# Output tiles of 128 tokens, and row pairs of w2 and m2 on one partition

## The chip, the cores and the metric

One core of a Trainium2 chip runs the whole kernel: TensorE (PE) multiplies, VectorE (DVE), ScalarE (ACT) and GpSimd (POOL) do the rest, SyncE (SP) issues most transfers between HBM and the core's 128-partition SBUF. The metric is device time in microseconds (us) of one execution, lower being better.

## The reference

Three parts follow each other. Attention of 32 packed queries over 576 tokens, then of the tokens over the packed result (4 batches, 8 heads of 64). Then a mixture of 4 experts with dense routing on the 2304 tokens x of width 512. Then a "soft" mixture: every token is spread over 32 slots, 8 experts work on 4 slots each, and each token reads the slots back.

```python
# x: (2304, 512) after attention; w1: (4,512,1024), w2: (4,1024,512)
p = domain_probs / (domain_probs.sum(-1, keepdims=True) + 1e-09)
for e in range(4):
    h = np.maximum(x @ w1[e], 0.0)
    out += p[:, e:e + 1] * (h @ w2[e])
x = out
# phi: (512, 32), m1: (8,512,1024), m2: (8,1024,512)
logits = x @ phi
d = softmax(logits, over tokens)
slot_input = (d.T @ x).reshape(8, 4, 512)
for e in range(8):
    h = np.maximum(slot_input[e] @ m1[e], 0.0)
    slot_out[e] = h @ m2[e]
c = softmax(logits, over slots)
return c @ slot_out          # (2304, 512)
```

All arrays are float32. In the kernel, m1 and m2 are the last part's `moe2_w1` and `moe2_w2`.

## The kernel before

The main loop computes the hidden layer h of the first mixture, 256 of its 1024 columns at a time, and never forms x: since slot_input is linear in h, h's columns are summed over tokens with the weights d (into `tacc`, 32 slots x 1024 columns x 4 experts), and w2 is applied to those sums alone. phi is folded into w2 beforehand (`wphi`). This loop ends at about 444 us; d's weights for the last batch and the last sums end at about 457 us.

What follows works on 32 slots, so it has little arithmetic and much weight to read:

- `tacc` is transposed (L961), and its two halves are added into `tt` (L973, L974).
- si = tt times w2 (L989), over 16 chunks of 512 KB.
- si is scaled and transposed (`sit`, L1007); hid = relu(si times m1) (L1026), over 32 chunks. `hidt` (L1047) transposes hid.
- so = hid times m2 (L1074): for the first four experts in all 512 output columns, over 16 chunks of 512 KB; for the last four in two parts (PARTS: 384 output columns, then 128), over 16 chunks of 384 KB and 4 of 512 KB.
- For each part, so is added up (L1094), spread by a selection matrix (`sr`, L1096), split into a rounded value and its remainder (`rr`, L1098, L1099), and multiplied with the turned c (`ct`) to give output rows (`o`, L1112). The PSUM results are drained by ACT and DVE in turn (L1065) into SBUF tiles `ob`, each stored by one DMA (L1119).

All weights of this end come as one list, `chunks` (L663 to L686): w2, m1, m2. Each chunk goes into the next of a ring of slots (4 KB per partition; some were `hn`, the main loop's buffer, and are named so in the trace, others are `ck`). `load_chunk` issues chunk after chunk on SP's queue in the order of the list, as slots come free: SP waits until the reader of the slot's former chunk is done. The output tiles take further slots of the same ring, and their stores come behind all chunks on SP's queue; the last one goes by ACT's queue.

`turn_c` (L637) makes ct. It is stepped once after each four chunks of hid's loop (L1037), so that its work lies between hid's matmuls: a matmul spreads a batch's 32-token blocks to 128 partitions, ACT rounds them into ct, and DVE writes the remainder on half of the partitions.

In the kernel before, an output tile is one batch's 96 rows r, of 6 tokens j each (token 6 r + j of the batch). A block x of 32 tokens (one of NBLK = 18) holds the tokens 18 t + x, so ct's row r = 3 t + y, and turn_c writes its columns with a step of 3. The order around the change is that of the code, by hand: nothing is scheduled.

Of the kernel before, what the change touches and what calls it, by code (L numbers as in the profile page):

```python
# [9 lines left out]
F32 = mybir.dt.float32  # L10
F32R = mybir.dt.float32r
AF = mybir.ActivationFunctionType
ALU = mybir.AluOpType
# [5 lines left out]
def tile_packed_attention_moe_softmoe(  # L19
# [21 lines left out]
    NBLK = S // 32  # L41
# [7 lines left out]
    EPS = 1e-9  # L49
    CHUNK = 1024  # L50
    PARTS = ((0, 384), (384, 128))
    NJ = NBLK // 3
    XC = CHUNK // 256
    HT_BUFS = 5
    NR = 5
# [49 lines left out]
    def tr_ps(name):  # L105
        turns["tr"] += 1
        return ps_tr[turns["tr"] % 2].tile([128, 512], F32, tag="tr", name=name)
# [529 lines left out]
    def turn_c(ct):  # L637
        cf = soft.tile([128, S], F32, tag="sx", name="cf", bufs=2).rearrange(
            "p (x t) -> p x t", t=32
        )  # L640
        dve.transpose(out=cf, in_=c_sb)
        for b in range(NB):
            own = slice(32 * b, 32 * b + 32)
            for y0, ny in ((0, 2), (2, 1)):
                m = ny * NJ * 32
                ps = tr_ps(f"ct{b}{y0}")
                pe.matmul(
                    ps[:, :m], fold[own].rearrange("p c t -> p (c t)"),
                    cf[own, NJ * y0 : NJ * (y0 + ny), :],
                    start=True, stop=True, tile_position=(32 * b, 0),  # L650
                )
                src = ps[:, :m].rearrange("p (y j t) -> p y j t", y=ny, t=32)
                dst = ct[:, b].rearrange("p j (t y) -> p y j t", y=3)[:, y0 : y0 + ny]
                for y in range(ny):
                    act.copy(dst[:, y], src[:, y])
                    for r in (slice(32, 64), slice(96, 128)):
                        dve.tensor_tensor(
                            out=dst[r, y], in0=src[r, y],
                            in1=dst[r, y].bitcast(F32), op=ALU.subtract,
                        )  # L660
                yield

    chunks = []  # L663
    for x in range(0, NFT, 2):
        for e in range(NE):
            chunks.append(
                w2[e, 128 * x : 128 * x + 256, :].rearrange("(x p) d -> p x d", p=128)
            )
    for s in range(NX // 4):
        for dc in range(NDC):  # L670
# [2 lines left out]
    for x in range(0, NFT, 2):  # L673
        for e in range(4):
            chunks.append(
                m2[e, 128 * x : 128 * x + 256, :].rearrange("(x p) d -> p x d", p=128)
            )
    for d0, dw in PARTS:
        nx = CHUNK // dw
        for x in range(0, NFT, nx):  # L680
            for e in range(4):
                chunks.append(
                    m2[4 + e, 128 * x : 128 * (x + nx), d0 : d0 + dw].rearrange(
                        "(x p) d -> p x d", p=128
                    )
                )  # L686
    chunk_t = {}
    slots = []
# [48 lines left out]
    with tc.manual_schedule():  # L737
# [214 lines left out]
        for t in st2:  # L952
            pool.memset(t, 0.0)
        tt = wphi
        ct = fin.tile([128, NB, NJ, 96], F32R, name="ct")
        for i in range(2):
            ps, ps2 = tr_ps(f"tt{i}a"), tr_ps(f"tt{i}b")
            for j in range(4):
                o = 128 * (4 * (2 * i + j // 2) + j % 2)
                for el in range(2):  # L960
                    pe.transpose(  # L961
                        (ps if j < 2 else ps2)[:, 256 * (j % 2) + 128 * el :][:, :128],
                        tacc[:, o + 256 * el : o + 256 * el + 128],
                        ident,
                    )
            for k, t in enumerate((ps, ps2)):
                t = t.rearrange("p (j l r q) -> p r j l q", j=2, l=2, r=2)
                both = tt[:, 4 * i + 2 * k : 4 * i + 2 * k + 2, :].rearrange(
                    "p j (a l s) -> p j l a s", a=2, l=2
                )  # L970
                for el in range(2):
                    dst = both[:, :, el]
                    act.copy(dst, t[:, 0, :, el].rearrange("p j (a s) -> p j a s", a=2))  # L973
                    dve.tensor_tensor(  # L974
                        out=dst, in0=t[:, 1, :, el].rearrange("p j (a s) -> p j a s", a=2),
                        in1=dst, op=ALU.add,
                    )
# [65 lines left out]
        for i in range(2):  # L1043
            ps = tr_ps(f"hidt{i}")
            for j in range(4):
                o = 512 * i + 128 * j
                pe.transpose(ps[:, 128 * j : 128 * j + 128], hid[:, o : o + 128], ident)  # L1047
            for s in range(2):
                (act.copy if i else dve.tensor_copy)(
                    hm[s][:, 4 * i : 4 * i + 4, :, 4 * s : 4 * s + 4].rearrange(  # L1050
                        "p a b c -> p (a b) c"
                    ),
                    ps.rearrange("p (a c) -> p a c", c=32)[:, :, 4 * s : 4 * s + 4],
                )
# [35 lines left out]
        for d0, dw in PARTS:  # L1090
            so = mm_ps(f"so{d0}")
            project(so, 1, dw)
            h = slice(d0, d0 + dw)
            dve.tensor_tensor(out=so_sb[:, h], in0=so[:, :dw], in1=so_sb[:, h], op=ALU.add)  # L1094
            sr = tr_ps(f"sr{d0}")
            pe.matmul(sr[:, :dw], sel, so_sb[:, h], start=True, stop=True)  # L1096
            rr = fin.tile([128, dw], F32R, name=f"rr{d0}")
            act.copy(rr, sr[:, :dw])  # L1098
            dve.tensor_tensor(  # L1099
                out=rr[64:128], in0=sr[64:128, :dw], in1=rr[64:128].bitcast(F32),  # L1100
                op=ALU.subtract,
            )
            nb, nt = 512 // dw, min(CHUNK // dw, NJ)
            for b in range(NB):
                rows = out[b * S : (b + 1) * S, h].rearrange("(r j) d -> r j d", j=NJ)
                for j0 in range(0, NJ, nt):
                    ob = out_tile()
                    for j in range(j0, j0 + nt, nb):
                        m = min(nb, j0 + nt - j)
                        ps = mm_ps(f"o{d0}_{b}_{j}")  # L1110
                        for jl in range(m):
                            pe.matmul(  # L1112
                                ps[:96, dw * jl : dw * jl + dw], ct[:, b, j + jl, :], rr,
                                start=True, stop=True,
                            )
                        drain(
                            ob[:96, dw * (j - j0) : dw * (j - j0 + m)], ps[:96, : dw * m]
                        )
                    (act if (d0, b) == (PARTS[-1][0], NB - 1) else sp).dma_start(  # L1119
                        rows[:, j0 : j0 + nt, :],  # L1120
                        ob[:96, : dw * nt].rearrange("p (j d) -> p j d", d=dw),
                    )


# [28 lines left out]
```

## Time and profile before

| | |
|---|---|
| Time, median of 3 runs | 549.1 us (548.97 to 549.73) |
| The profiled execution's own time | 549.31 us |
| its span, first to last instruction | 547.2 us |
| PE busy | 498.7 us, 91% |
| DVE, ACT, POOL busy | 322.2, 240.0, 236.3 us |
| moved by DMA | 104.06 MB, of which 4.72 MB written |

The busy shares are means over stages with different limits. Nearly all of PE's work lies in the main loop; the stage after it is read from its own stretch. A row of the view by stage has, after the stretch, its length, busy time and count for each engine, then TensorE's granted clock, the DMA engines' busy share and the rate. A share can read a little over 1, since packets overlap.

### The profile page before, as it was taken

To read this page: it belongs to the slowest core of one execution; us is meant where nothing else is said; L and a number is where in the kernel's file an instruction comes from. 1 tells how busy PE (TensorE), PEld (TensorE's weight loads), DVE (VectorE), ACT (ScalarE), POOL (GpSimd) and SP (SyncE) were. 2 spreads that over 40 slices of the span, in tenths; PEclk is the share of its full clock that TensorE was granted. 3 is DMA by queue.
4 is the path that set the end of the run, shared out by engine and by line. 5 is a ranking of instruction groups with operands and counts; after the bars stand their busy time and mean duration, and the time that the engine had idled before them with its cause. 6 is when DMAs were issued, how large, how long until landed. Compare 5 with 4: busy or idle time off the path is not lost.

```text
span 547.2 us, 12839 instructions
## 1 busy us (share of the span) xinstructions
PE 498.7 (91%) x5356; PEld 347.5 (63%) x5356; DVE 322.2 (59%) x623; ACT 240.0 (44%) x548; POOL 236.3 (43%) x246
## 2 busy tenths in 40 slices
PE   7898999989999999899998989999999977998882
PEld 5776787867865767687556768775787853222132
DVE  6475457776767776768776676666645434451051
ACT  3766564655452447365334654551454411120041
POOL 8212445676642557675335555842555612000000
PEclk9998999999999999999999999999999997998998
DMA  8997155352430443443205432360388369999998
GB/s 283 365 375 271 49 166 176 98 166 79 153 122 1 146 143 103 150 148 120 79 10 177 158 100 79 132 234 22 126 277 292 128 238 398 409 389 383 371 253 239
DMA packets 70874, 104.06 MB, mean 190 GB/s; under 512 B 4433, under 2 KB 50257, under 8 KB 70817
## 3 DMA queue, kind: packets, MB, share of 16 engines
q1 hardware_dynamic: 66992, 93.20, 49.2%
q0 software_dynamic: 3232, 9.75, 6.0%
q8 instruction: 42, 0.69, 0.5%
q10 hardware_dynamic: 592, 0.29, 0.2%
q14 instruction: 16, 0.12, 0.1%
HBM read 98.52 MB, written 4.72 MB: 189 GB/s over the span
## 4 chain that ended last, share of the span: by engine, by line
PE 54%; DVE 15%; DMA 14%; ACT 8%; issue 4%; POOL 3%; SPq 0%; POOLq 0%; DVEq 0%; ACTq 0%
PE h L473 26%; DMA ck<-in_moe_w_dram 7%; PE sl L611 6%; PE g L443 5%; PE lg L500 4%; DMA hn<-in_moe_w_dram 3%; DVE pkt L366 3%; PE sb L297 3%; ACT etm L336 3%; DMA k<-in_k_dram 3%; PE sa L297 2%; PE w2t L251 2%; DVE hn L483 2%; POOL hn L484 2%; PE pw L237 1%
## 5 line engine op out<-in xcount | busy, mean ns | idle before, releaser
L473 PE MATMUL h<-a,g 128*128 128x288 f32 x1536 | 227.6, 302 | 6.9 <-DVE g L455 4.5
L473 PEld LDWEIGHTS h<-a,g 128*128 128x128 f32 x1536 | 208.7, 188 | 33.4 <-issue 22.3
L484 POOL TENSOR_TENSOR hn<-hn,dp_sb 128x576 f32<-128x576 f32 x128 | 152.0, 1193 | 130.0 <-DVE hn L483 126.3
L477 ACT ACTIVATE ht<-h 128x288 f32<-128x288 f32 x256 | 103.7, 412 | 155.2 <-PE h L473 154.9
L483 DVE STREAM_TRANSPOSE hn<-ht 128x576 f32<-128x576 f32 x128 | 96.3, 758 | 50.2 <-ACT ht L477 50.0
L455 DVE TENSOR_TENSOR g<-g,g 128x512 fp32r<-128x512 f32 x64 | 41.1, 683 | 24.8 <-ACT g L454 24.8
L611 PE MATMUL sl<-hn,dpt 32*32 32x512 f32 x1152 | 48.2, 597 | 2.4 <-DVE dpt L572 2.0
L454 ACT CAST g<-g 128x512 fp32r<-128x512 f32 x64 | 34.3, 588 | 21.1 <-PE g L443 21.0
L500 PE MATMUL lg<-ht,wphi 128*32 128x288 f32 x512 | 37.8, 412 | 0.0
L443 PE MATMUL g<-w,gl 64*32 64x512 f32 x512 | 35.7, 601 | 0.4 <-ACT ht L477 0.2
L611 PEld LDWEIGHTS sl<-hn,dpt 32*32 32x32 f32 x1152 | 21.0, 103 | 22.3 <-issue 13.3
L500 PEld LDWEIGHTS lg<-ht,wphi 128*32 128x32 f32 x512 | 13.5, 109 | 32.7 <-issue 25.5
L366 DVE COPY pkt<-gl 32x32 f32<-32x32 f32 x64 | 22.8, 356 | 7.3 <-ACT gl L357 6.5
L346 PE MATMUL pv<-etm,v 128*64 128x64 f32 x468 | 19.0, 225 | 6.5 <-ACT etm L336 3.4
L410 POOL TENSOR_TENSOR a<-a,a 64x576 fp32r<-64x576 f32 x14 | 20.0, 1427 | 9.6 <-ACT a L409 8.8
L336 ACT COPY etm<-et 32x288 f32<-32x288 f32 x52 | 22.2, 428 | 1.6 <-DVE et L330 0.4
L346 PEld LDWEIGHTS pv<-etm,v 128*64 128x64 f32 x468 | 16.2, 137 | 10.6 <-ACT etm L336 5.7
L1074 PE MATMUL so<-hn,tacc 128*32 128x384 f32 (+1 forms) x80 | 18.5, 590 | 2.7 <-DMA hn<-in_moe_w_dram 2.5
L629 DVE TENSOR_TENSOR tacc<-sl,tacc 128x512 f32<-128x512 f32 (+2 forms) x32 | 15.3, 545 | 9.4 <-PE sl L611 9.4
L297 PE MATMUL sa<-k,pt 128*128 128x288 f32 x56 | 16.9, 428 | 3.7 <-DVE k L288 3.6
L256 ACT COPY hn<-w2t 128x512 f32<-128x512 f32 x32 | 17.3, 588 | 6.6 <-PE w2t L251 6.5
L251 PE MATMUL w2t<-ident,hn 128*128 128x128 f32 x128 | 18.3, 287 | 1.8 <-ACT hn L256 1.3
(180 smaller groups left out, 492.4 us busy)
## 6 DMA issues: line engine op xcount, KB each, us to landing
w<-in_moe_w_dram SPq DMA_DIRECT2D x32, 1024.0 KB, 5.4
hn<-in_moe_w_dram SPq DMA_DIRECT2D x42, 512.0 KB, 9.7
ck<-in_moe_w_dram SPq DMA_DIRECT2D x42, 512.0 KB, 8.0
hn<-in_moe_w_dram SPq DMA_DIRECT2D x14, 384.0 KB, 8.5
q<-in_q_dram POOLq DMA_DIRECT2D x12, 288.0 KB, 3.2
out_dram<-ob SPq DMA_DIRECT2D x11, 288.0 KB, 4.4
k<-in_k_dram POOLq DMA_DIRECT2D x10, 288.0 KB, 3.2
v<-in_v_dram POOLq DMA_DIRECT2D x10, 288.0 KB, 3.6
```

Of the source, the lines that this page charges most:

```text
L297: pe.matmul(ps[:, :HS], lhs[:, j, :], t[:, :, j, :], start=(j == 0), stop=(j == 1))
L336: act.copy(etb[hf % len(etb)][r, h % 2, :, 32 * (h // 2) : 32 * (h // 2) + 32], et[r, HB * hf : HB * hf + HB, :],)
L346: pe.matmul(pv[64 * par : 64 * par + 64, :64], vn[:, x, :], etb[hf % len(etb)][:, par, x, :], start=(hf == 0 and x == 0), stop=(hf == 1 an ...
L366: dve.tensor_copy(pkb[32 * h : 32 * h + 32, dh, o : o + 32], glb[src : src + 32, 2 * g + h // 2, :],)
L443: pe.matmul(pss[g][32 * ((c + 2 * g) % 4) : 32 * ((c + 2 * g) % 4) + 32, :], gl[b % 2][r, c, :], t[r, c], start=True, stop=True, tile_posi ...
L455: dve.tensor_tensor(out=lo, in0=pss[g], in1=hi.bitcast(F32), op=ALU.subtract)
L473: pe.matmul(ps[:, :HS], gg[:, l, g, e % 2, fs], r[:, ts], start=(g == 0 and t == 0), stop=(g == 1 and t == 2),)
L477: act.activation(out=ht[:, ts], in_=ps[:, :HS], func=AF.Relu)
L483: dve.transpose(out=own, in_=unturned.pop((n, kf, e)).rearrange("p (x t) -> p x t", t=32))
L484: pool.tensor_tensor(out=own, in0=own, in1=dp_sb[:, n // NU, :, e].unsqueeze(2).to_broadcast([128, NBLK, 32]), op=ALU.mult,)
L500: pe.matmul(lg_t[b, pr][32 * c : 32 * c + 32, :HS], wphi[:, 2 * i + kf, 32 * e : 32 * e + 32], ht_t[n, kf, e][:, HS * hf : HS * hf + HS], ...
L611: pe.matmul(pss[f][c : c + 32, :], dpt[r, x, :], hn[r, p0 : p0 + NU, x, 2 * ep : 2 * ep + 2].rearrange("p n e k f -> p n (e k f)"), start= ...
```

## The change

The diff does three things.

1. An output tile holds 128 rows: 32 tokens t of each of the 4 batches, for a fixed x; partition 32 b + t of tile x is token 18 (32 b + t) + x. ct is laid out as 18 blocks of 128 columns, and `turn_c` makes it in pieces of 9 blocks instead of 12 and 6. There are 18 blocks instead of 24 for the last matmuls; a stored tile has 2 blocks of 384 columns or 6 of 128 (OUT_X).
2. In a chunk of w2 or m2, partition p holds rows next to each other in HBM (w2: rows 2 p and 2 p + 1 of the chunk's 256; m2: two of the rows 8 p to 8 p + 7, or all eight of them for the 128-column part), instead of rows p and p + 128.
3. The transposes of tacc and hid take their columns with a step of 2 and of 8, so that the same rows meet.

```diff
--- before.py
+++ after.py
@@ -49,7 +49,7 @@
     EPS = 1e-9
     CHUNK = 1024
     PARTS = ((0, 384), (384, 128))
-    NJ = NBLK // 3
+    OUT_X = {384: 2, 128: 6}
     XC = CHUNK // 256
     HT_BUFS = 5
     NR = 5
@@ -641,30 +641,28 @@
         dve.transpose(out=cf, in_=c_sb)
         for b in range(NB):
             own = slice(32 * b, 32 * b + 32)
-            for y0, ny in ((0, 2), (2, 1)):
-                m = ny * NJ * 32
-                ps = tr_ps(f"ct{b}{y0}")
+            for x0 in range(0, NBLK, HB):
+                m = HB * 32
+                ps = tr_ps(f"ct{b}{x0}")
                 pe.matmul(
                     ps[:, :m], fold[own].rearrange("p c t -> p (c t)"),
-                    cf[own, NJ * y0 : NJ * (y0 + ny), :],
+                    cf[own, x0 : x0 + HB, :],
                     start=True, stop=True, tile_position=(32 * b, 0),
                 )
-                src = ps[:, :m].rearrange("p (y j t) -> p y j t", y=ny, t=32)
-                dst = ct[:, b].rearrange("p j (t y) -> p y j t", y=3)[:, y0 : y0 + ny]
-                for y in range(ny):
-                    act.copy(dst[:, y], src[:, y])
-                    for r in (slice(32, 64), slice(96, 128)):
-                        dve.tensor_tensor(
-                            out=dst[r, y], in0=src[r, y],
-                            in1=dst[r, y].bitcast(F32), op=ALU.subtract,
-                        )
+                src = ps[:, :m].rearrange("p (x t) -> p x t", t=32)
+                dst = ct[:, x0 : x0 + HB, own]
+                act.copy(dst, src)
+                for r in (slice(32, 64), slice(96, 128)):
+                    dve.tensor_tensor(
+                        out=dst[r], in0=src[r], in1=dst[r].bitcast(F32), op=ALU.subtract
+                    )
                 yield
 
     chunks = []
     for x in range(0, NFT, 2):
         for e in range(NE):
             chunks.append(
-                w2[e, 128 * x : 128 * x + 256, :].rearrange("(x p) d -> p x d", p=128)
+                w2[e, 128 * x : 128 * x + 256, :].rearrange("(p x) d -> p x d", x=2)
             )
     for s in range(NX // 4):
         for dc in range(NDC):
@@ -673,16 +671,16 @@
     for x in range(0, NFT, 2):
         for e in range(4):
             chunks.append(
-                m2[e, 128 * x : 128 * x + 256, :].rearrange("(x p) d -> p x d", p=128)
+                m2[e].rearrange("(p x) d -> p x d", x=NFT)[:, x : x + 2, :]
             )
     for d0, dw in PARTS:
         nx = CHUNK // dw
         for x in range(0, NFT, nx):
             for e in range(4):
                 chunks.append(
-                    m2[4 + e, 128 * x : 128 * (x + nx), d0 : d0 + dw].rearrange(
-                        "(x p) d -> p x d", p=128
-                    )
+                    m2[4 + e, :, d0 : d0 + dw].rearrange("(p x) d -> p x d", x=NFT)[
+                        :, x : x + nx, :
+                    ]
                 )
     chunk_t = {}
     slots = []
@@ -952,15 +950,15 @@
         for t in st2:
             pool.memset(t, 0.0)
         tt = wphi
-        ct = fin.tile([128, NB, NJ, 96], F32R, name="ct")
+        ct = fin.tile([128, NBLK, 128], F32R, name="ct")
         for i in range(2):
             ps, ps2 = tr_ps(f"tt{i}a"), tr_ps(f"tt{i}b")
             for j in range(4):
-                o = 128 * (4 * (2 * i + j // 2) + j % 2)
                 for el in range(2):
+                    o = 512 * (2 * i + j // 2) + 256 * el
                     pe.transpose(
                         (ps if j < 2 else ps2)[:, 256 * (j % 2) + 128 * el :][:, :128],
-                        tacc[:, o + 256 * el : o + 256 * el + 128],
+                        tacc[:, o : o + 256].rearrange("p (f x) -> p x f", x=2)[:, j % 2],
                         ident,
                     )
             for k, t in enumerate((ps, ps2)):
@@ -1043,8 +1041,11 @@
         for i in range(2):
             ps = tr_ps(f"hidt{i}")
             for j in range(4):
-                o = 512 * i + 128 * j
-                pe.transpose(ps[:, 128 * j : 128 * j + 128], hid[:, o : o + 128], ident)
+                pe.transpose(
+                    ps[:, 128 * j : 128 * j + 128],
+                    hid.rearrange("p (f x) -> p x f", x=NFT)[:, 4 * i + j],
+                    ident,
+                )
             for s in range(2):
                 (act.copy if i else dve.tensor_copy)(
                     hm[s][:, 4 * i : 4 * i + 4, :, 4 * s : 4 * s + 4].rearrange(
@@ -1100,26 +1101,23 @@
                 out=rr[64:128], in0=sr[64:128, :dw], in1=rr[64:128].bitcast(F32),
                 op=ALU.subtract,
             )
-            nb, nt = 512 // dw, min(CHUNK // dw, NJ)
-            for b in range(NB):
-                rows = out[b * S : (b + 1) * S, h].rearrange("(r j) d -> r j d", j=NJ)
-                for j0 in range(0, NJ, nt):
-                    ob = out_tile()
-                    for j in range(j0, j0 + nt, nb):
-                        m = min(nb, j0 + nt - j)
-                        ps = mm_ps(f"o{d0}_{b}_{j}")
-                        for jl in range(m):
-                            pe.matmul(
-                                ps[:96, dw * jl : dw * jl + dw], ct[:, b, j + jl, :], rr,
-                                start=True, stop=True,
-                            )
-                        drain(
-                            ob[:96, dw * (j - j0) : dw * (j - j0 + m)], ps[:96, : dw * m]
+            nb, nt = 512 // dw, OUT_X[dw]
+            rows = out[:, h].rearrange("(p x) d -> p x d", x=NBLK)
+            for x0 in range(0, NBLK, nt):
+                ob = out_tile()
+                for x in range(x0, x0 + nt, nb):
+                    m = min(nb, x0 + nt - x)
+                    ps = mm_ps(f"o{d0}_{x}")
+                    for xl in range(m):
+                        pe.matmul(
+                            ps[:, dw * xl : dw * xl + dw], ct[:, x + xl, :], rr,
+                            start=True, stop=True,
                         )
-                    (act if (d0, b) == (PARTS[-1][0], NB - 1) else sp).dma_start(
-                        rows[:, j0 : j0 + nt, :],
-                        ob[:96, : dw * nt].rearrange("p (j d) -> p j d", d=dw),
-                    )
+                    drain(ob[:, dw * (x - x0) : dw * (x - x0 + m)], ps[:, : dw * m])
+                (act if d0 and x0 + nt == NBLK else sp).dma_start(
+                    rows[:, x0 : x0 + nt, :],
+                    ob[:, : dw * nt].rearrange("p (x d) -> p x d", d=dw),
+                )
 
 
 # ---- launch: one core; inputs and outputs as the reference has them ----
```

The order of the instructions moves in three places. On SP's queue before, near the end of the chunk list (the second number of a shape is rows per partition, `hn` and `ck` are slots):

```order
L715 DMA hn<-in_moe_w_dram 128x2x512 x4
L715 DMA ck_5750<-in_moe_w_dram 128x2x512 x2
L715 DMA ck_5753<-in_moe_w_dram 128x2x512 x2
L715 DMA ck_5784<-in_moe_w_dram 128x2x512 x2
L715 DMA ck_5787<-in_moe_w_dram 128x2x512
L715 DMA ck_5807<-in_moe_w_dram 128x2x512
L715 DMA ck_5809<-in_moe_w_dram 128x2x512 x2
L715 DMA hn<-in_moe_w_dram 128x2x512 x2
L715 DMA hn<-in_moe_w_dram 128x2x384 x14
```

and the same place after:

```order
L713 DMA hn<-in_moe_w_dram 128x1024 x4
L713 DMA ck_5750<-in_moe_w_dram 128x1024 x2
L713 DMA ck_5753<-in_moe_w_dram 128x1024 x2
L713 DMA ck_5784<-in_moe_w_dram 128x1024 x2
L713 DMA ck_5787<-in_moe_w_dram 128x1024
L713 DMA ck_5804<-in_moe_w_dram 128x1024
L713 DMA ck_5806<-in_moe_w_dram 128x1024 x2
L713 DMA hn<-in_moe_w_dram 128x1024 x2
L713 DMA hn<-in_moe_w_dram 128x2x384 x14
```

Counts and order are the same; the first 16 chunks of m2 are now one run of 1024 elements per partition, those of 384 columns keep two runs.

On SP's queue before, the output stores that follow the chunks (`ob` and `hn` are output tiles):

```order
L1119 DMA out_dram<-ob_6021 96x2x384
L1119 DMA out_dram<-ob_6029 96x2x384
L1119 DMA out_dram<-ob_6037 96x2x384
L1119 DMA out_dram<-hn 96x2x384 x4
L1119 DMA out_dram<-ob_6073 96x2x384 x2
L1119 DMA out_dram<-ob_6088 96x2x384 x2
L1119 DMA out_dram<-ob_6103 96x2x384
L1119 DMA out_dram<-ob_6103 576x1x128
L1119 DMA out_dram<-ob_6161 576x1x128
L1119 DMA out_dram<-ob_6173 576x1x128
```

and after:

```order
L1117 DMA out_dram<-ob_6009 128x2x384
L1117 DMA out_dram<-ob_6017 128x2x384
L1117 DMA out_dram<-ob_6025 128x2x384
L1117 DMA out_dram<-hn 128x2x384 x4
L1117 DMA out_dram<-ob_6061 128x2x384 x2
L1117 DMA out_dram<-ob_6115 128x6x128 x2
```

Fifteen stores from 96 partitions become eleven from 128; in the 128-column part before, the tokens of a batch form one list of 576 rows.

On ACT, before, its half of the drains of the 128-column part, with the last store on its own queue:

```order
L1098 CAST rr_6147<-sr_6145 128x128
L1065 COPY ob_6103<-o_0_0_6150 96x512
L1065 COPY ob_6161<-o_1_0_6162 96x512
L1065 COPY ob_6173<-o_2_0_6174 96x512
L1065 COPY ob_6185<-o_3_0_6186 96x512
L1119 DMA out_dram<-ob_6185 576x1x128
```

and after:

```order
L1099 CAST rr_6112<-sr_6110 128x128
L1066 COPY ob_6115<-o_0_6116 128x512
L1066 COPY ob_6115<-o_6_6127 128x512
L1066 COPY ob_6138<-o_12_6139 128x512
L1117 DMA out_dram<-ob_6138 128x6x128
```

Four pieces of 512 columns become three, and the last store stands behind the third.

## Rows read from the trace of the kernel before

**Rows 1.** The page, 40 equal slices: busy tenths of the DMA engines and GB/s.
```profile
DMA  8997155352430443443205432360388369999998
GB/s 283 365 375 271 49 166 176 98 166 79 153 122 1 146 143 103 150 148 120 79 10 177 158 100 79 132 234 22 126 277 292 128 238 398 409 389 383 371 253 239
```

**Rows 2.** Chain of waits, 420 to 548 us: start us, length us, what.
```profile
464.64 7.36 DMA ck<-in_moe_w_dram
...
513.47 8.48 DMA ck<-in_moe_w_dram
...
534.26 4.36 DMA out_dram<-ob
```

**Rows 3.** Busy time by stage, the last two columns being DMA share and GB/s.
```profile
464.00:480.00 16.00, 14.75 (x122) 4.76 (x118) 6.26 (x21) 2.01 (x5) 2.17 (x2) 1.00 1.03 409
482.00:502.00 20.00, 18.47 (x131) 5.67 (x130) 7.88 (x19) 3.91 (x10) 0.00 (x0) 0.91 1.05 387
505.00:518.00 13.00, 11.12 (x52) 2.53 (x56) 0.00 (x0) 0.59 (x1) 0.00 (x0) 1.00 1.07 373
522.00:526.00 4.00, 2.39 (x12) 0.67 (x12) 0.90 (x2) 0.48 (x1) 0.00 (x0) 1.00 1.00 257
530.00:540.00 10.00, 7.46 (x101) 5.34 (x99) 5.37 (x13) 4.95 (x11) 0.00 (x0) 1.00 0.98 291
541.00:546.00 5.00, 0.00 (x0) 0.00 (x0) 0.00 (x0) 0.00 (x0) 0.00 (x0) 0.64 0.86 221
```

**Rows 4.** DMA issues from 447 to 522 us: count, KB each, median us to landing.
```profile
ck<-in_moe_w_dram SPq DMA_DIRECT2D x23, 512.0 KB, 10.4
hn<-in_moe_w_dram SPq DMA_DIRECT2D x21, 512.0 KB, 10.2
hn<-in_moe_w_dram SPq DMA_DIRECT2D x14, 384.0 KB, 8.5
ck<-in_moe_w_dram SPq DMA_DIRECT2D x2, 384.0 KB, 8.5
```

**Rows 5.** DMA packets in three stretches: 505 to 518, 530 to 540, 104 to 106.
```profile
DMA packets 3354, 4.85 MB, mean 373 GB/s; under 512 B 198, under 2 KB 3354, under 8 KB 3354
...
DMA packets 2041, 2.91 MB, mean 291 GB/s; under 512 B 155, under 2 KB 2040, under 8 KB 2040
...
DMA packets 732, 0.75 MB, mean 374 GB/s; under 512 B 2, under 2 KB 732, under 8 KB 732
```

**Rows 6.** Timeline of the output stage: start us, length us, engine, line, what.
```profile
526.27 6.37 PE L1112 MATMUL o<-rr,ct 128*96 128x384 f32 x24 [1.16 <-DVE rr L1099]
...
527.52 1.38 SPq L1119 DMA_DIRECT2D out_dram<-ob  x3
...
532.57 1.96 PE L1074 MATMUL so<-ck,tacc 128*32 128x128 f32 x64
...
536.11 2.46 PE L1112 MATMUL o<-rr,ct 128*96 128x128 f32 x24 [0.68 <-DVE rr L1099]
```

**Rows 7.** Groups by line and form, 455 to 524 us: count, busy us, mean ns, idle.
```profile
L657 DVE TENSOR_TENSOR ct<-ct,ct 32x192 fp32r<-32x192 f32 x24 | 10.6, 440 | 9.9 <-ACT ct L655 9.5
...
L989 PE MATMUL si<-ck,wphi 128*32 128x512 f32 x48 | 8.2, 695 | 0.0
...
L1047 PEld LDWEIGHTS hidt<-ident,wphi 128*128 128x128 f32 x8 | 1.1, 178 | 2.0 <-ACT wphi L1041 1.2 <-PE hidt L1047 0.8
...
L961 PEld LDWEIGHTS tt0b<-ident,tacc 128*128 128x128 f32 x4 | 0.9, 230 | 0.0
```

**Rows 8.** Waits of SP's queue, 440 to 548 us: total, times, longest.
```profile
SPq L715 <- PE si L989: 4.1, 4, 3.1
SPq L715 <- PE hidt L1047: 0.2, 1, 0.2
```

**Rows 9.** DVE's drains of the 384-column output part, by form, 520 to 548 us.
```profile
L1065 DVE COPY ob<-o 96x384 f32<-96x384 f32 x8 | 4.2, 549 | 0.8 <-PE o L1112 0.7
```

**Rows 10.** DMA rate in 40 slices of 541 to 546 us.
```profile
GB/s 217 213 209 258 266 221 238 262 233 242 254 274 279 315 315 303 287 238 188 238 291 254 250 258 234 221 262 246 197 176 193 225 213 180 184 156 115 66 37 21
```

## The prediction, made before the result was known

> **What bounds the kernel now.** I read the strip of 40 slices first [rows 1]. After the first few, the slices show the DMA engines between idle and full by turns. From the 34th, at about 450 us, they are full to the end. The edits touch only what runs in or just before that last stretch, so I then read the chain of waits there [rows 2]. Six long pieces nearly without a gap are waits on a weight DMA, from 464.64 to 521.95 us (the first and the sixth are shown). A short chain of compute (so, sr, rr, o) follows, and the last long piece, 4.36 us at 534.26, is an output store. So the tail is a queue of transfers, and its time is bytes divided by rate, stretch by stretch.
>
> The rates come from the busy-time table by stage [rows 3]: 409 GB/s at 464 to 480 us, 387 at 482 to 502, 373 at 505 to 518, 257 at 522 to 526, 291 at 530 to 540, 221 at 541 to 546. The DMA share is 0.98 to 1.07 in all but the last: the engines do not starve, they are slow per byte. What is moved in each stretch follows from the order of the chunk list and the issue counts [rows 4]: 23 + 21 + 14 + 2 = 60 chunks are issued from 447 us on. The list has 84: 16 of w2, 32 of m1, 16 of m2's first four experts, 16 of the 384-column part and 4 of the 128-column part of the others. So the 60 are 24 of m1 and all of m2, and w2 has been issued before. So the first stretch is m1 in rows of 4 KB, the second m2 in rows of 2 KB, the third m2 in pieces of 384 columns (1.5 KB; 4.85 MB / 3354 packets = 1.45 KB) [rows 5], the fourth m2's 128 columns (512 B), the fifth stores of 384 columns (2.91 MB / 2041 = 1.43 KB), the last stores of 128.
>
> **The change, part by part.**
>
> *m2, first four experts.* Partition p now takes two neighbouring rows, so a chunk is 128 runs of 4 KB in place of 256 of 2 KB. Bytes: 16 x 524,288 = 8.39 MB. At 387 GB/s this is 21.7 us, at m1's 409 GB/s 20.5 us: -1.2 us. The bounds are 0 (the rate stays 387) and -1.2; I take -1.2, because the m1 stretch shows the same queue, destination and size per DMA. All of it lies on the chain, since the PE waits on these DMAs.
>
> *m2, the other four experts.* Packets stay 1.5 KB and 512 B; only the spacing of the rows in HBM changes. I take 0. Below zero: 6.29 MB at 387 instead of 373 would be -0.6 us. Above zero see the second rival. The 512 B chunks are read while the chain from so to the first store runs (521.96 to 527.52) [rows 2, 6], so a change there is hidden unless they take over 1 us longer.
>
> *w2.* Also 4 KB runs, but these 16 chunks are in SBUF before si asks for them (PE idled 0.0 us ahead of 48 of its 64 matmuls) [rows 7], and the queue has free slices until 447 [rows 1]. 0.
>
> *Transposes of tacc and hid.* The same 16 and 8 matmuls, whose weights are now read with a step of 2 and of 8 elements. The trace of before shows no such read, so its price may be nothing. Now a weight load takes 230 ns and 178 ns [rows 7]; three times that, a wide guess, would add 16 x 0.46 = 7.4 us ahead of si and 8 x 0.36 = 2.8 us ahead of so. The work that hides it is the transfer queue: SP waits on si 4.1 us and on hidt 0.2 us [rows 8], yet the engines stay full, because each chunk lands 10.2 to 10.4 us after its issue [rows 4]. So about 6 us more at si and 10 at hidt are covered. I take 0; past the cover, 1.3 us at most.
>
> *Turning c (ct).* 12 casts of 192 columns become 8 of 288, and 24 subtractions 16. The subtractions are 24 x 440 ns = 10.6 us now [rows 7]. If they go by columns the sum stays (16 x 660 ns), if by count it is 16 x 440 ns = 7.0. Either way it lies beside m1's transfers, on engines that mostly wait: 0.
>
> *The output stage.* Sixteen stores of 288 KB from 96 partitions become twelve of 384 KB from 128, and 24 drains of 384 columns become 18; of the narrow part's 8, 6 are left. A drain's time goes by columns (549 ns on DVE) [rows 9], not by partitions, so the first store is ready as long after the last m2 chunk as now. The 384-column part is 12 x 294,912 = 3.54 MB. It now moves at 291 GB/s: 12.2 us. What a store from 128 partitions does, the trace does not show. One bound is 291 again. The other is 373, the read of equal packets over 128 partitions. Per packet, 16 engines x share x time / packets [rows 3, 5] is 16 x 1.07 x 13 us / 3354 = 66 ns there and 16 x 0.98 x 10 us / 2041 = 77 ns in the store. I take 373. It is the nearest row with 128 partitions, and reads of w1 in pieces of 1 KB, one from each 4 KB row, run at 374 too at 104 to 106 us [rows 5]: the rate hardly depends on the address pattern there. That gives 9.5 us: -2.7 us.
>
> [...]
>
> The 128-column part is 1.18 MB: at 221 GB/s 5.3 us. Its nearest row with 128 partitions is the 512 B read at 522 to 526 us, 257 GB/s [rows 3]: 4.6 us, -0.7 us. Bounds: 0 and, at the 315 of the best slices [rows 10], -1.6.
>
> What is late next: from the first o matmul, 18 drains take 9 x 0.55 = 5.0 us on DVE (12 x 0.55 = 6.6 now). The narrow part needs 3.5 us from its first so matmul to its first o matmul (532.57 to 536.11) [rows 6], and about 0.9 us for a tile: 9.4 us. The store queue starts 1.25 us after the first o matmul (526.27 to 527.52) and has 9.5 us of wide tiles: 10.7 us. So the first narrow tile is ready 1.3 us before the queue runs dry. At a much faster store rate it would be the next wait.
>
> Sum: -1.2 - 2.7 - 0.7 = -4.6 us on the profiled execution's 549.3 us (span 547.2): 544.7. Its runs have a median 0.2 us lower, so 544.5.
>
> **The rivals.**
>
> *Stores have a rate of their own.* HBM writes, not partitions, hold 291 GB/s. For it: there is no store from 128 partitions in the trace, and in the stores' stretch the engines are busy 0.98 of the time already. Against it: packets equal in size take 66 ns when read. Then only m2 pays: 547.9.
>
> *The new spacing slows the reads, and the kernel ends slower.* Neighbouring partitions of m2 now start 16 KB apart, in place of 2 KB. Price: m2's 8.39 and 6.29 MB now take 21.7 + 16.9 = 38.6 us. Their rate would have to fall below 14.68 MB / (38.6 + 3.4) us = 350 GB/s to eat the stores' gain. For it: the 512 B pieces, whose reads skip most of each row, fall to 257. Against it: the 1 KB pieces 4 KB apart at 374. With 315, midway between these two: 46.6 us, +8.0 - 3.4 = +4.6: 553.7.
>
> [...]
>
> *The longer m2 runs bring nothing*, the engines being limited by something other than packet size there: 545.7.
>
> *The change moves nothing that counts*, both rates staying: 549.1.
>
> **How the numbers follow.** Forecast 58%, m2 without gain 10%, stores without gain 17%, nothing 5%, slower reads 10%. The forecast's own range is 542.6 (with -0.6 for the wide m2 reads, -0.9 more for narrow stores and 0.4 for the spread of runs) to 546.5 (stores at about 325 GB/s). The range goes on to 548.4, which takes in the stores without gain; left out are the slower reads, the 5% and small tails. About 0.2%, 1.1 us, is what a measurement of this kernel can tell from no change. The stores-without-gain case, at 1.2 us, is half on each side of that. Faster: 58 + 10 + 10 = 78%; same 12%; slower 10%.
>
> **What would show it.** m2's stretch at about 409 GB/s with half the packets; stores at about 370 with twelve issues of 384 KB; the DMA share full from 448 us on. Wrong would be: stores still near 291; m2's stretches under 373; a wait of so on hidt or of the narrow stores on the drains in the chain, with the DMA share below 0.9 beside it.

## The result, and the profile after

The changed kernel takes 543.84 us (median of 4 runs, 543.35 to 545.67) against 549.41 (4 runs, 548.97 to 550.19): a ratio of 0.9902, 95% interval 0.9882 to 0.9922, so 5.4 us less by the ratio. 544.5 was predicted. Two later comparisons of the same two kernels gave 0.9934 (0.9907 to 0.9961) and 0.9934 (0.9909 to 0.9959): 3.6 us. The profiled execution took 543.35 us, its span 541.6.

The busy time by stage of the kernel after [rows 3] holds the answer; DMA share and GB/s are the last two columns. The rows are m1, m2 of the first four experts, m2's 384 columns, its 128 columns, the wide stores and the narrow stores.

```profile
462.00:478.00 16.00, 14.76 (x109) 4.58 (x101) 5.82 (x20) 1.48 (x3) 2.31 (x2) 0.89 1.03 409
480.00:498.00 18.00, 15.75 (x106) 5.32 (x102) 5.70 (x14) 2.82 (x8) 0.00 (x0) 0.91 1.03 409
505.00:516.00 11.00, 9.27 (x46) 2.23 (x46) 0.00 (x0) 0.00 (x0) 0.00 (x0) 1.00 1.07 373
520.00:524.00 4.00, 2.12 (x8) 0.94 (x6) 1.17 (x3) 0.70 (x2) 0.00 (x0) 1.00 1.12 278
527.00:534.00 7.00, 5.88 (x89) 4.62 (x88) 3.18 (x8) 2.88 (x7) 0.00 (x0) 1.00 1.03 361
535.00:539.00 4.00, 0.00 (x0) 0.00 (x0) 0.00 (x0) 0.00 (x0) 0.00 (x0) 0.50 1.04 293
```

The second row is now like the first: 409 in place of 387. The third is still 373. The wide stores run at 361 in place of 291, the narrow ones at 293 (before 221, over a stretch that takes in the end of the stores). Packets of the second and fifth stretch, from the DMA view of the same kernel [rows 5]:

```profile
DMA packets 2014, 7.35 MB, mean 409 GB/s; under 512 B 223, under 2 KB 223, under 8 KB 2012
...
DMA packets 1730, 2.53 MB, mean 361 GB/s; under 512 B 95, under 2 KB 1729, under 8 KB 1729
```

7.35 MB / 2014 is 3.65 KB a packet, where the kernel before had 2 KB rows. A store's packet takes 16 x 1.03 x 7 us / 1730 = 67 ns, against 77 ns before.

The chain of waits of the kernel after [rows 2]; the first column is the start:

```profile
442.88 9.74 PE sl L611 x271
...
461.92 9.45 DMA ck<-in_moe_w_dram
...
510.58 8.41 DMA ck<-in_moe_w_dram
```

It is made of the same waits. The last wide chunk of m2 lands at 518.99 us, before at 521.95; from there to the end of the span it is 22.6 us, before 25.3. The timeline of the output stage [rows 6]:

```profile
523.30 4.98 PE L1112 MATMUL o<-rr,ct 128*128 128x384 f32 x18 [1.16 <-DVE rr L1100]
...
524.57 1.53 SPq L1117 DMA_DIRECT2D out_dram<-ob  x3
...
528.22 1.95 PE L1075 MATMUL so<-ck,tacc 128*32 128x128 f32 x64
...
531.76 2.23 PE L1112 MATMUL o<-rr,ct 128*128 128x128 f32 x18 [0.69 <-DVE rr L1100]
```

The first store is issued 1.27 us after the first o matmul (before 1.25), and the wide drains are done in 5.0 us of matmuls instead of 6.4. From that first issue to the end it is 17.0 us instead of 19.7. Turning c and the weights of the transposes, groups by line and form in 454 to 522 us [rows 7], and SP's waits [rows 8]:

```profile
L656 DVE TENSOR_TENSOR ct<-ct,ct 32x288 fp32r<-32x288 f32 x16 | 7.3, 457 | 14.9 <-ACT ct L654 14.8
...
L1044 PEld LDWEIGHTS hidt<-ident,wphi 128*128 128x128 f32 x8 | 1.5, 221 | 2.7 <-issue 2.7
...
L959 PEld LDWEIGHTS tt0b<-ident,tacc 128*128 128x128 f32 x4 | 0.9, 226 | 0.0
```

```profile
SPq L713 <- PE si L987: 1.2, 2, 0.8
...
SPq L713 <- PE hidt L1044: 0.2, 1, 0.2
```

The weight load of tt0b, now with a step of 2, takes 226 ns, before 230, at a granted clock of 0.50 both times. That of hidt, with a step of 8, takes 221, before 178, but more of it now falls where the granted clock is 0.50. Two of the runs below have all eight at a clock of 1.00: 193 ns with the step of 8 (half_low) and 140 without it (stores_only). So there the step costs 53 ns a load, 0.4 us in all, beside a DMA queue whose share stays at 1.03. SP waits for si less than before, for hidt as long.

### The profile page after: what moved, and what is told of

The parts are those of the page before. It is cut to its first block, busy times and chain, and to the rows that moved or that the text cites. A ratio compares the mean times of both kernels' runs of the same rounds, so it can differ in the third digit from the quotient of the medians.

```text
span 541.6 us, 12780 instructions
## 1 busy us (share of the span) xinstructions
PE 494.4 (91%) x5344; PEld 346.5 (64%) x5344; DVE 316.7 (58%) x611; ACT 235.9 (44%) x540; POOL 236.0 (44%) x246
## 4 chain that ended last, share of the span: by engine, by line
PE 54%; DVE 15%; DMA 14%; ACT 8%; issue 4%; POOL 3%; SPq 0%; POOLq 0%; DVEq 0%; ACTq 0%
PE h L473 26%; DMA ck<-in_moe_w_dram 7%; PE sl L611 6%; PE g L443 5%; PE lg L500 5%; DMA hn<-in_moe_w_dram 3%; DVE pkt L366 3%; PE sb L297 3%; ACT etm L336 3%; DMA k<-in_k_dram 2%; PE w2t L251 2%; PE sa L297 2%; DVE hn L483 2%; POOL hn L484 2%; PE pw L237 1%
## 5 line engine op out<-in xcount | busy, mean ns | idle before, releaser
L483 DVE STREAM_TRANSPOSE hn<-ht 128x576 f32<-128x576 f32 x128 | 96.3, 758 | 50.2 <-ACT ht L477 50.1
L346 PE MATMUL pv<-etm,v 128*64 128x64 f32 x468 | 19.1, 225 | 7.1 <-ACT etm L336 4.0
L346 PEld LDWEIGHTS pv<-etm,v 128*64 128x64 f32 x468 | 16.2, 137 | 11.2 <-ACT etm L336 5.7
L297 PE MATMUL sa<-k,pt 128*128 128x288 f32 x56 | 16.5, 420 | 3.4 <-DVE k L288 3.3
```

The lines of the kernel that those rows point to most:

```text
L297: pe.matmul(ps[:, :HS], lhs[:, j, :], t[:, :, j, :], start=(j == 0), stop=(j == 1))
L346: pe.matmul(pv[64 * par : 64 * par + 64, :64], vn[:, x, :], etb[hf % len(etb)][:, par, x, :], start=(hf == 0 and x == 0), stop=(hf == 1 an ...
L483: dve.transpose(out=own, in_=unturned.pop((n, kf, e)).rearrange("p (x t) -> p x t", t=32))
```

## The experiments

Three questions were open: what share each half of the change has, why a store from 128 partitions is faster, and where the rest of the 5.4 us comes from, since the two terms seen in the trace (-1.2 for m2 by its rates, -2.7 in the output stage) sum to -3.9.

**stores_only.** Output tiles of 128 tokens, with the chunks and transposes of before. From the changed kernel:

```diff
-  w2[e, 128 * x : 128 * x + 256, :].rearrange("(p x) d -> p x d", x=2)
+  w2[e, 128 * x : 128 * x + 256, :].rearrange("(x p) d -> p x d", p=128)
...
-  m2[e].rearrange("(p x) d -> p x d", x=NFT)[:, x : x + 2, :]
+  m2[e, 128 * x : 128 * x + 256, :].rearrange("(x p) d -> p x d", p=128)
...
```

Expected: 

> Output tiles of 128 tokens alone; chunks of w2 and m2 and the transposes as before. Theory (the gain is two separate transfer rates, stores and m2): the wide stores run at about 361 GB/s as in the changed kernel, m2's first half stays at 387, and the time is 549.4 - 2.7 (first store issue to end: 19.7 us before, 17.0 after) = 546.7 us. Rival (the 5.6 us of the whole change come mainly from w2 and m2, including the 1.3 us by which the main loop ended earlier): 548.4 or more. Rival (the stores are faster only because the queue of chunks before them is faster): stores near 291 GB/s, 549.4.

Measured: 546.96 us against 549.42, ratio 0.9947 (0.9927 to 0.9968), so 2.9 us less. By stage (m2's first half, its 384 columns, the wide stores):

```profile
484.00:502.00 18.00, 16.41 (x125) 5.12 (x118) 5.16 (x13) 2.42 (x7) 0.00 (x0) 1.00 1.05 386
506.00:519.00 13.00, 10.77 (x48) 2.37 (x48) 0.00 (x0) 0.59 (x1) 0.00 (x0) 1.00 1.07 373
532.00:538.00 6.00, 4.90 (x84) 3.94 (x83) 2.48 (x7) 2.08 (x5) 0.00 (x0) 1.00 1.03 361
```

The stores have 361 behind a queue that is as slow as before (386, 373): the first theory holds, and the store rate does not come from the chunks.

**pairs_only.** The same lines the other way: the kernel before with the row pairs and the strided transposes, output tiles of 96 rows.

Expected: 

> Row pairs of w2 and m2 alone; output tiles of 96 rows as before. Theory: m2's first half runs at about 409 GB/s in 4 KB packets, the wide m2 reads stay at 373, stores stay near 291, and the time is 549.4 - 1.2 = 548.2 us; the main loop, which this edit does not touch before 345 us, ends with the same scatter as any other run, so its 1.3 us are not part of it. Rival (the row pairs also shorten something in the main loop): 546.9, with the last sums (sl) starting near 442.9 us in every profile that has the pairs and near 444.1 in every one that has not.

Measured: 547.10, ratio 0.9955 (0.9938 to 0.9971): 2.5 us less, where 1.2 was expected and the interval begins at 1.6. The same three stages:

```profile
480.00:498.00 18.00, 15.83 (x110) 5.35 (x103) 9.05 (x21) 4.32 (x11) 0.00 (x0) 0.91 1.03 408
505.00:516.00 11.00, 9.40 (x46) 2.23 (x46) 0.00 (x0) 0.00 (x0) 0.00 (x0) 1.00 1.07 373
528.00:536.00 8.00, 6.32 (x96) 4.83 (x95) 4.30 (x10) 3.91 (x9) 0.00 (x0) 1.00 0.97 292
```

The rates are those of the theory: 408, 373, and stores at 292. From the last wide chunk's landing to the end it is 25.3 us, as before. The rates account for 1.2 us; the other 1.3 are not explained by any stage that the edit touches. While the last sums ran, chunks came faster in this profile than in the first one of the changed kernel, which has the same pairs; the rate at 450 to 452 us, of pairs_only and then of the kernel after:

```profile
450.00:452.00 2.00, 2.00 (x84) 1.60 (x67) 0.00 (x0) 0.00 (x0) 0.00 (x0) 1.00 1.01 412
```

```profile
450.00:452.00 2.00, 2.00 (x78) 1.27 (x54) 0.00 (x0) 0.00 (x0) 0.00 (x0) 1.00 0.95 340
```

So the pairs are not what makes them fast there. The last sums began at 442.17 us in this profile, 2.0 us earlier than in the kernel before, as the rival asked, but their start moves in profiles of one and the same kernel too (next). The rates and the earlier start together are 3.2 us, and so is the difference of the two spans (544.1 and 547.2 us); but these sums also took 11.2 us instead of 9.7, and why that cost nothing is not shown. Of the other nine runs there is no profile, so the 1.3 us stay open.

**both_again, both_third.** The changed kernel once more, beside other kernels on one chip.

Expected of the first: 

> The whole change once more, beside the two halves on one chip. Theory: the two halves add up, 549.4 - 2.7 - 1.2 = 545.5 us, and what the first comparison showed beyond that (543.8) is where the half-speed stretch of TensorE's clock fell in the prologue: the start of the last sums (sl) then varies by about 1.3 us from profile to profile, whatever the kernel. Rival: the whole is more than its halves, 543.8 again while the halves give 546.7 and 548.2.

Measured: 546.23, ratio 0.9934. That is near the 545.5 of the two added terms, not the 543.8 of the first comparison. The halves as measured, 2.9 and 2.5 us, sum to 5.4, where the whole gave 3.6 in the same comparison. Their intervals (1.8 to 4.0, 1.6 to 3.4 and 2.1 to 5.1 us) are too wide to say whether something is lost between them. In this profile the last sums began at 443.59 us, in the first of the same kernel at 442.88, in both_third at 442.14: the start moves by 1.4 us with nothing changed. Most of it goes with the granted clock, the third column from the end. The stretch of 50 to 60 us of the kernel before, and then of the kernel after:

```profile
50.00:60.00 10.00, 9.18 (x106) 8.30 (x107) 5.42 (x20) 4.74 (x10) 2.44 (x3) 0.83 0.31 99
```

```profile
50.00:60.00 10.00, 8.94 (x113) 7.83 (x113) 6.94 (x22) 5.22 (x12) 3.02 (x3) 1.00 0.35 116
```

At 0.83 the clock was at 0.50 for a part of that stretch (51 to 54 us), and the last sums began at 444.13; in the other it was at 1.00 throughout. Before, the fall came at 51 us. PE had been busy for 1.46 of the 3 us from 48 to 51, but for as much of the 3 from 49 to 52 in the kernel after, where no fall followed, so what brings it on is not shown. After, there was one at 16 us (0.50 from 16 to 19), where it cost nothing: from the first matmul of pv (L346) to the first of sb (L297) it is 10.8 us in both (13.83 to 24.65 and 14.42 to 25.24). Of eleven profiles, the six with the fall at 51 to 52 us have sums that begin at 443.6 to 444.3, and four of the five without it 442.1 to 442.9; the fifth, half_low, began at 444.26, but its main loop had begun late. The first matmul of h and the last sums, of the kernel before, the kernel after and half_low:

```profile
48.11 0.38 PE L473 MATMUL h<-a,g 128*128 128x288 f32 x1
444.13 9.74 PE sl L611 x271
...
48.69 0.38 PE L473 MATMUL h<-a,g 128*128 128x288 f32 x1
442.88 9.74 PE sl L611 x271
...
50.15 0.38 PE L473 MATMUL h<-a,g 128*128 128x288 f32 x1
444.26 9.74 PE sl L611 x269
```

From the one to the other it is 396.0, 394.2 and 394.1 us; over all eleven profiles, 395.3 to 396.0 with the fall and 394.0 to 394.2 without it. So the fall costs 1.1 to 2.0 us, and the rest is when the loop begins (47.9 to 50.2 us). Both profiles without the row pairs have this fall, and four of the nine with them, which is too few to say whether the change moves it. The last sums themselves differ as well, as groups by line of stores_only and then of the kernel after:

```profile
L611 PE MATMUL sl<-hn,dpt 32*32 32x512 f32 x288 | 11.3, 690 | 2.0 <-DVE dpt L572 2.0
```

```profile
L611 PE MATMUL sl<-hn,dpt 32*32 32x512 f32 x288 | 9.7, 597 | 2.0 <-DVE dpt L572 2.0
```

690 ns against 597 for the same matmuls: 1.6 us. The clock over 443 to 453 us, stores_only and then the kernel after, was

```profile
443.00:453.00 10.00, 9.19 (x241) 5.78 (x248) 0.77 (x2) 0.04 (x1) 0.00 (x0) 0.83 0.38 119
```

```profile
443.00:453.00 10.00, 9.62 (x288) 5.90 (x284) 0.39 (x1) 0.00 (x0) 0.18 (x1) 1.00 0.64 226
```

0.83 and 1.00, so a part at 0.50 in the first and none in the second (ahead of it, from 440 to 444, PE was busy for 1.99 of the 4 us in the one and 2.00 in the other); the queue of chunks then starts later too, since SP waits for these sums to free slots (8.7 us in the kernel after, 10.3 in stores_only). In pairs_only, whose sums had such a fall, the chunks were not late, so this price is not paid each time. Such stretches fall differently in executions of one kernel, and 1.1 to 2.0 us and 1.6 us are a large part of the scatter of 4 us that its runs show. The kernel after, as first profiled, had neither; the kernel before had the first alone.

Expected of the third: 

> The changed kernel beside cut_320, to have both on one chip, and as a further look at the scatter. By the theory that the half-speed stretches of TensorE's clock make the scatter, the last sums take 9.7 us where none of them falls in, and 11.3 where one does; from the last wide m2 chunk's landing to the end it is 22.6 us in either case. Time: 545.4, the median of all its runs so far.

Measured: 544.52 against 547.98, ratio 0.9934. The sums took 9.7 us, as they should without a fall in them. From the last wide chunk to the end it was 23.1 us and not 22.6: the clock was at 0.50 for 3.4 us from 523.7 us on, and the first matmuls of o were slow.

**half_low, half_mid, three_quarters.** The changed kernel, each store writing only a part of the tile's partitions, the rest of the output not being stored. For half_low:

```diff
-  rows[:, x0 : x0 + nt, :],
-  ob[:, : dw * nt].rearrange("p (x d) -> p x d", d=dw),
+  rows[0:64, x0 : x0 + nt, :],
+  ob[0:64, : dw * nt].rearrange("p (x d) -> p x d", d=dw),
```

half_mid has 32:96 and three_quarters 0:96 in both places.

Expected of half_low: 

> The changed kernel, but each output store writes only partitions 0 to 63 of its tile (half of the output is not stored). [...] Rival (the rate goes by the bytes of a store or by the spacing of its rows in HBM, which is 36 KB here as in the changed kernel): about 350 GB/s, limited by the drains, and about 13 us. Rival (it goes by the number of partitions alone): the same as half_mid.

Expected of half_mid: 

> As half_low, but each store writes partitions 32 to 95 (again half of the output, with the same bytes, packets and spacing). [...] Rival (bytes or spacing): the same 350. Rival (number of partitions alone): as slow as half_low, whatever that is.

Expected of three_quarters: 

> As half_low, but each store writes partitions 0 to 95 (a quarter of the output is not stored), 288 KB like the stores of the kernel before, with rows 36 KB apart as in the changed kernel instead of 12 KB. [...] Rival (spacing in HBM made the difference): about 361.

Measured in 530 to 534 us, wide stores, for half_low, then half_mid, then three_quarters (one execution of each):

```profile
530.00:534.00 4.00, 3.59 (x71) 2.65 (x70) 2.17 (x5) 1.36 (x3) 0.00 (x0) 1.00 1.00 200
```

```profile
530.00:534.00 4.00, 3.40 (x70) 2.54 (x69) 1.92 (x4) 1.26 (x4) 0.00 (x0) 1.00 0.81 286
```

```profile
530.00:534.00 4.00, 3.59 (x71) 2.56 (x70) 2.40 (x6) 1.58 (x4) 0.00 (x0) 1.00 1.01 309
```

Two stores with equal bytes, packets, partition counts and addresses' spacing run at 200 GB/s from partitions 0 to 63 and at 286 from 32 to 95. In the second the engines are busy 0.81 of the time: its nine wide stores of 196,608 bytes were issued from 526.67 to 532.28 us, one every 0.70 us, which is 280 GB/s. 286 / 0.81 would be 353. So neither the number of partitions nor HBM's spacing sets the difference, but which partitions they are. 0 to 95 gives 309 with the spacing of the changed kernel, a little above the 291 of the kernel before (so a small effect of the spacing is not excluded), and far from 361. What makes 0 to 63 slower than 32 to 95 is not shown. From the first issue to the end it was 14.4 us in half_mid and 15.4 in half_low, where about 13 was expected of half_low if bytes or spacing set the rate.

**even_parts.** Since the reads' rates here go by packet size (409 GB/s at 4 KB, 373 at 1.5 KB, 278 at 512 B in the kernel after), the 512 B packets of the 128-column part were the next suspect. From the changed kernel:

```diff
-  PARTS = ((0, 384), (384, 128))
-  OUT_X = {384: 2, 128: 6}
+  PARTS = ((0, 256), (256, 256))
+  OUT_X = {256: 3}
```

Expected: 

> The changed kernel with the 512 output columns of the last four experts cut into 256 and 256 instead of 384 and 128, so that m2's second half and all stores move in packets of 1 KB. Theory (the tail is bytes over rate, and the rate goes by packet size: 374 GB/s for 1 KB reads, about 278 for 512 B reads, 361 for 1.5 KB stores, 285 for 512 B stores): reads 8.39 MB / 374 = 22.4 us, during which the first part's chain is hidden; stores 4.72 MB / 360 = 13.1 us with the second chain (5.6 us) under the first part's 6.6 us; 36.7 us from the first such read to the end against 16.9 + 22.6 = 39.5 now: 2.8 us less than the changed kernel, about 542.4 us where both_again had 546.2 on this chip, or 543.4 by the middle of both its measurements. Rival (the second chain is not covered, since the stores of the first part are done before it ends): no gain, 545 to 546.

Measured: 544.24 against 548.81, ratio 0.9916 (0.9897 to 0.9935); not to be told from the changed kernel (0.9934, 0.9907 to 0.9961 in both_again, which ran on another chip, so only the ratios compare). The stages around the second chain (so to o):

```profile
506.00:526.00 20.00, 14.77 (x101) 7.37 (x104) 3.33 (x8) 3.79 (x7) 0.00 (x0) 0.74 1.08 347
526.00:530.00 4.00, 3.16 (x51) 1.63 (x44) 0.00 (x0) 0.00 (x0) 0.00 (x0) 1.00 1.09 377
530.00:532.00 2.00, 1.11 (x4) 0.30 (x2) 0.42 (x1) 0.34 (x1) 0.00 (x0) 1.00 0.83 291
532.00:534.00 2.00, 1.25 (x8) 1.04 (x9) 1.21 (x3) 0.94 (x3) 0.00 (x0) 1.00 0.23 81
534.00:536.00 2.00, 1.93 (x12) 1.38 (x11) 1.27 (x3) 1.79 (x5) 0.00 (x0) 1.00 0.71 237
```

Reads of 1 KB have 347, not 374, and a gap stands before the second part's stores: 0.17 + 0.77 + 0.29 of 2 us each, 2.5 us. The last read lands at 528.5 us and the gap begins near 531, though the first part's 2.36 MB of stores alone would take 6.6 us at 360. By the rates from 528.5 us on, about 1.3 MB of them were left then (an estimate); the other 1.0 MB had run beside the last reads. So the second chain stands bare for the most part, as the rival had it.

**cut_320.** A cut between the two:

```diff
-  PARTS = ((0, 384), (384, 128))
-  OUT_X = {384: 2, 128: 6}
+  PARTS = ((0, 320), (320, 192))
+  OUT_X = {320: 3, 192: 3}
+  ROWS = {512: 2, 320: 2, 192: 4}
...
-  nx = CHUNK // dw
+  nx = ROWS[dw]
```

Expected: 

> The changed kernel with the output columns of the last four experts cut into 320 and 192. Theory (bytes over rate plus the stretches in which no transfer is ready): reads 5.24 MB at about 360 GB/s and 3.15 MB at about 320, stores 2.95 MB at 350 and 1.77 MB at 310, 38.5 us, against 38.4 for the cut at 384 by its own rates; what is left to win is the gap ahead of the first store (the DMA share was 0.52 for 2 us with the cut at 384, about 1 us), and the second chain lies under 8.4 us of stores. So 0 to 1 us less than the changed kernel on the same chip, with a DMA share near 1 at both places. Rival (as with the cut at 256 the stores of the first part run ahead of the last reads, and the second chain stands bare): a gap of 2 us or more before the narrow stores, and no gain.

Measured: 542.18 (541.18 to 542.62) against 547.98, ratio 0.9884 (0.9857 to 0.9912), beside both_third's 0.9934 from the same comparison; no run of the one overlaps the other's. It is the fastest kernel here, by 2.3 us against the changed one, more than the expected 0 to 1. Its stages (the third row is the stretch around the first store), and then both_third's:

```profile
504.00:514.00 10.00, 8.76 (x44) 2.11 (x39) 0.00 (x0) 0.58 (x1) 0.00 (x0) 1.00 1.07 363
518.00:522.00 4.00, 2.21 (x13) 0.81 (x14) 0.99 (x2) 0.43 (x1) 0.00 (x0) 1.00 1.11 327
522.00:528.00 6.00, 5.92 (x38) 4.37 (x42) 4.24 (x9) 3.67 (x9) 0.00 (x0) 0.72 1.08 354
528.00:532.00 4.00, 2.71 (x55) 1.61 (x45) 0.72 (x2) 0.32 (x1) 0.00 (x0) 1.00 1.06 386
532.00:534.00 2.00, 1.80 (x13) 1.46 (x13) 1.12 (x4) 1.43 (x4) 0.00 (x0) 1.00 0.62 226
534.00:538.00 4.00, 1.30 (x6) 1.06 (x6) 1.00 (x3) 1.25 (x3) 0.00 (x0) 0.54 1.04 324
```

```profile
518.00:522.00 4.00, 2.77 (x14) 0.81 (x14) 0.56 (x1) 0.00 (x0) 0.00 (x0) 1.00 1.04 270
524.00:528.00 4.00, 4.00 (x14) 3.07 (x14) 2.86 (x6) 2.82 (x6) 0.00 (x0) 0.62 0.58 190
536.00:540.00 4.00, 0.00 (x0) 0.00 (x0) 0.00 (x0) 0.00 (x0) 0.00 (x0) 0.66 1.03 288
```

Narrow packets of 768 B have 327 GB/s for reads and 324 for stores, where 512 B have 270 and 288. The gap ahead of the first store (share 0.58 over 4 us; 0.52 over 2 us in the first profile of the kernel after) is gone: 1.08 from 522 to 528 us. One of 0.38 x 2 us is left ahead of the narrow stores. The stores at 528 to 532 us are faster than those of the changed kernel (361), though their packets are shorter, as the DMA view of cut_320 for that stretch shows (1.24 KB a packet):

```profile
DMA packets 1242, 1.54 MB, mean 386 GB/s; under 512 B 48, under 2 KB 1241, under 8 KB 1241
```

Why is open, and it is what my expectation lacked. The same shows in even_parts: its 1 KB stores moved 378 GB/s from 528.5 to 531 us, behind the last reads, and 338 from 535 to 541. So packet size alone does not set a store's rate.

## Why the prediction was right

*m2's first four experts, -1.2.* Right in size: 387 to 409 GB/s in packets of 4 KB, in every profile with the pairs.

*m2's last four, 0.* Right: 373 before and after, with rows 16 KB apart. So the rival of slower reads falls.

*Wide stores, -2.7.* Right in mechanism, 361 instead of the 373 taken: 3.54 MB in 9.8 us, so -2.4. So the rival of a store rate of its own falls, and half_low and half_mid show that it is the covered partitions (200 GB/s from 0 to 63, 286 from 32 to 95); why is not shown.

*Narrow stores, -0.7.* 1.18 MB at 293 take 4.0 us and not 4.6, but the end is longer. Slices of 0.125 us of the stores' last stretch, 535 to 540 us, of the kernel after [rows 10]:

```profile
GB/s 381 340 332 299 287 299 291 254 213 205 258 352 328 287 279 295 291 303 291 291 299 279 303 291 303 283 295 303 275 291 287 291 303 291 287 180 66 25 20 20
```

From 539.5 us hardly anything moves, and the span ends at 541.6, 2.1 us later; before, the rate fell under 70 at 545.6 and the span ended 1.6 us later. Wide, narrow and end together gave -2.7 where -3.4 was summed. So this term was a little too large.

*What was taken at 0* (w2, the transposes, ct, the drains): nothing of it shows on the chain, though the step of 8 has a price (193 ns a load against 140). 16 subtractions of 288 columns took 7.3 us, the lower of the two estimates. A drain of 384 columns on DVE took 554 ns with 128 partitions, 549 with 96. What was "late next" was placed rightly: there is no gap ahead of the narrow stores, share 1.02 to 1.04 from 526 to 538 us.

*The sum.* -4.6 was forecast; the stages give -3.9, the later comparisons -3.6, the first -5.4. The forecast of 544.5 came near the first result partly by chance. The two profiled executions differ by 5.7 us in their spans: 3.9 are the stages, 1.25 the earlier start of the last sums, with the fall of the clock at 51 us before and not after, and 0.5 is not assigned; the sums themselves took 9.74 us in both. Of the other runs of that comparison there is no profile. The prediction had no term for this scatter.

## What to carry to other kernels

Where a stage is a queue of transfers, write its time as bytes over rate, stretch by stretch, and look for what sets each rate: here it was bytes per packet (reads from 257 GB/s at 512 B to 409 at 4 KB) and the partitions that a transfer covers (stores of 1.5 KB packets at 291 from 96 partitions, 361 from 128). Lay tiles over all 128 partitions even where 96 come more naturally from the problem. When one result of 1% is larger than the sum of the stages that can be seen, repeat it before explaining the rest.

## What the runs showed of the hardware that was not expected

- A store from 64 partitions ran at 200 GB/s (0 to 63, half_low) or 286 (32 to 95, half_mid; 353 per busy time), depending only on which 64.
- Stores in packets of 1.25 KB moved 386 GB/s (cut_320, 528 to 532 us), stores of 1.5 KB 361 in the changed kernel, stores of 1 KB 378 and then 338 in one execution (even_parts).
- TensorE's granted clock fell to 0.50 at places that differed between executions of the same kernel (51 us or not; 444 us or not). The fall at 51 us cost 1.1 to 2.0 us, the one in the last sums made them 1.6 us longer, and the one at 16 us cost nothing.
- A weight load with a step of 8 float32 took 193 ns at a granted clock of 1.00 (half_low), without a step 140 (stores_only).
- The rates of reads over 128 partitions, in GB/s: 257 to 278 (512 B), 327 (768 B), 347 in even_parts and 374 at 104 to 106 us (1 KB), 363 (1.25 KB), 373 (1.5 KB), 387 (2 KB), 409 (4 KB).
